# A hand-written instruction order re-planned from its last third on, with the last row tile stored in halves

## The chip, the cores and the metric

The kernel runs on one core of a Trainium2 chip. A core has five engines with an instruction stream each: TensorE (PE in the rows, its weight loads PEld), VectorE (DVE), ScalarE (ACT), GpSimd (POOL) and SyncE (SP), which here only issues DMAs. Each stream runs in order; between streams there are semaphores. The metric is device time in microseconds (us), from the first to the last instruction of the core and what lies around it. Three runs of the kernel before took 441.34, 442.01 and 442.62 us; the median, 442.01 us, is the time before.

## The reference

A linear attention and a feed-forward layer. What is computed, cut to its core:

```python
q_s = exp(q - max(q, -1));  q_s /= sum(q_s, -1) + 1e-9        # 8 x 8 x 576 x 64
k_s = exp(k - max(k, 2));   k_s /= sum(k_s, 2) + 1e-9
kv = einsum('bhsd,bhse->bhde', k_s, v)
x = einsum('bhsd,bhde->bhse', q_s, kv)                        # -> 4608 x 512
h = x @ w_in                                                  # 512 -> 1024
sm = exp(h - max(h, -1));   sm /= sum(sm, -1) + 1e-9
solu = h * sm
ln = (solu - mean) / sqrt(var + 1e-6) * g_ln
out = ln @ w_out                                              # 1024 -> 512
```

## The kernel before

The 4608 rows are 36 row tiles of 128 rows (`tiles`): four main tiles for each of the 8 batches, and one tile for each pair of batches that holds 64 remaining rows of both ("rests"). A tile's name is its batch and its place in it: `6_0` is tile 27, `7_2` is tile 33, `5_4` is tile 26 (a rest). float32 operands of the matmuls are split into a high and a low float16 part, and a product is three matmuls.

From tile 13 on, two tiles are one work (twins, `late_rests` too): `hidden_twin` computes the hidden layer of both with seven block products in place of eight (lines 726 to 784). A block product is 6 matmuls of 128x512 (L734). Of a twin, `t2` is the hidden tile of the second row tile and `t1` that of the first. The order is: product 11 onto `t2`, product 12 onto `t1`; a copy of `t2` (`vw`, L172 on ScalarE or L174 on VectorE); products s2 and s1; copies; s3 and s4; reduces on VectorE (L770, L772); the last product, 22 with t4, onto `t2`; its reduce (L777). There are two hidden tiles in PSUM at a time (`h`, two slots), so a twin's first product waits for the last read of the hidden tiles of the twin before: `L842` (in `hidden`, one tile) or `L939` (in `hidden_pair`, both tiles, one instruction each). Before `L842` stand, for its tile, the maximum (L772 or L777 and L779), its absolute value `am` (L829), `pi` (L832), its power `p` (L835, always POOL) and `ph` (L838); before `L939` the same for two tiles in 128x2 instructions (L919, L927, L929, L890, L935).

Five pairs (tiles 27, 29, 31, 33 and 26; `SPLIT_OUT`) are also projected by seven block products (`pair_products`, L1049, 12 matmuls of 128x256 each, three accumulators x, y, z) and scaled and stored by `pair_rows`. Other tiles are projected by `project` (L1113, 6 matmuls of 128x512 a step, 24 a tile). Between u and uT lies a DMA transpose on SP (L859, L898).

Nothing is scheduled by a tool: the table `ORDER` is a list of steps and `in_turns` runs one generator step for each, so the order in that list is the order in every engine's stream. `K6` is the next step of the keys of batch 6, `Q7a` of queries, `x27` of the attention of tile 27, `h22` of a tile's hidden layer after the products, `H27` of a twin's products, `U27` of `hidden_pair`, `O27` of its products, `E27` of its rows, `o20` of a tile's projection, `TO` of the blocks of the output weights (L1009 to L1021); `.v` puts the step's movable instruction on VectorE in place of its default, ScalarE or GpSimd, and `*3` repeats it. `SLOTS` says which buffer each tile takes.

`pair_rows` has 11 steps: rr; a copy of x; y plus that; four scalings; `scaled_onto` twice; `stored(1)` and, last, `stored(0)`, each one or two DMAs (two for a rest, of 64 rows).

Of the kernel before, what the change touches and what calls it, by code (L numbers as in the profile page):

```python
# [17 lines left out]
P = 128  # L18
# [5 lines left out]
REST_TWINS = 5, 7  # L24
SPLIT_OUT = (27, 29, 31, 33, 26)
# [78 lines left out]
def linear_attention_solu_ffn(ctx: ExitStack, tc: tile.TileContext, q, k, v, w_in, w_out, g_ln, out):  # L104
# [7 lines left out]
    nc = tc.nc  # L112
# [942 lines left out]
    def pair_rows(row_tiles):  # L1055
# [20 lines left out]
        def stored(i):  # L1076
            for rows, dst in destinations(row_tiles[i]):
                nc.sync.dma_start(out=dst, in_=out_rows[rows, i])
# [5 lines left out]
        scaled(0, right, "y")  # L1084
        yield
        scaled(0, left, "x")
        yield
        scaled(1, right, "y")
        yield
        scaled_onto(1)  # L1090
# [160 lines left out]
```

## Time and profile before

| | |
|---|---|
| median of three runs | 442.01 us (441.34 to 442.62) |
| the profiled execution | 440.85 us, of it the span 439.1 us, granted TensorE clock 0.997 |
| busy in the span | PE 417.4 us (95%), DVE 385.5 us (88%), ACT 323.4 us (74%), POOL 316.1 us (72%) |
| chain that ended last | PE 73%, POOL 8%, ACT 8%, DVE 6% |
| DMA | 77.93 MB; HBM read 36.70 MB, written 9.44 MB |

PE's busy share is read together with the views by stage: the first 66 us hold most of its idle time, and the end of the span, after the last matmul, the rest. A row of a timeline gives the start, the length, the engine and line, and, in brackets, how long the engine was idle just before and what ended that.

### The profile page before, as it was taken

What the parts mean: (1) busy time and instruction counts of PE and PEld (TensorE: products, weight loads), DVE (VectorE), ACT (ScalarE), POOL (GpSimd) and SP (SyncE); (2) the same over time, 40 slices, a digit from 0 to 9 for tenths busy, and PEclk for the clock granted to TensorE, in tenths of its full rate; (3) what the DMA queues carried; (4) which work ended last, traced back from release to release, by engine and by line L of the source; (5) the groups of instructions that cost most, each with busy time, mean ns of one, the idle gap of its engine ahead of it and who ended that gap; (6) DMA issues with size and microseconds to landing.
All of it is one profiled execution on the core that took longest, in us unless ns stands there. A gap on an engine that the chain in (4) does not pass through costs nothing.

```text
span 439.1 us, 9202 instructions
## 1 busy us (share of the span) xinstructions
PE 417.4 (95%) x3441; PEld 218.1 (50%) x3441; DVE 385.5 (88%) x765; ACT 323.4 (74%) x555; POOL 316.1 (72%) x336
## 2 busy tenths in 40 slices
PE   2798899999999999999999999999999999999995
PEld 1444344454454444544544445445444445666885
DVE  5999999999898998889988869999999998988952
ACT  3799998696796689878875677768685686785920
POOL 4206983889998879859966888886939897778340
PEclk9999999999999999999999999999999999999998
DMA  8989788489799696499996568994533665379982
GB/s 277 409 306 315 154 152 233 91 206 245 173 223 184 150 192 135 90 224 217 186 251 146 126 147 188 247 215 95 78 72 82 111 144 104 63 172 188 231 204 73
DMA packets 182620, 77.93 MB, mean 177 GB/s; under 512 B 162088, under 2 KB 171312, under 8 KB 182576
## 3 DMA queue, kind: packets, MB, share of 16 engines
q1 hardware_dynamic: 182576, 77.35, 77.0%
q8 instruction: 27, 0.44, 0.4%
q14 instruction: 17, 0.14, 0.1%
HBM read 36.70 MB, written 9.44 MB: 105 GB/s over the span
## 4 chain that ended last, share of the span: by engine, by line
PE 73%; POOL 8%; ACT 8%; DVE 6%; issue 3%; DMA 1%; ACTq 0%; POOLq 0%; DVEq 0%
PE o L1113 24%; PE h L734 18%; PE h L811 12%; PE kv L471 3%; PE x L666 3%; PE o_2y L1049 2%; PE o_0y L1049 2%; PE o_0x L1049 1%; PE o_2z L1049 1%; PE o_0z L1049 1%; PE o_2x L1049 1%; POOL qm L523 1%; POOL r L882 1%; POOL qhl L548 1%; POOL am L829 1%
## 5 line engine op out<-in xcount | busy, mean ns | idle before, releaser
L1113 PE MATMUL o<-wo,uT 128*128 128x512 f16 x624 | 141.4, 379 | 0.0
L1113 PEld LDWEIGHTS <-uT 128*128 128x128 f16 x624 | 60.3, 98 | 72.7 <-issue 1.6
L811 PE MATMUL h<-wi,xT 128*128 128x512 f16 x240 | 54.4, 379 | 0.0
L734 PE MATMUL h<-wt,split 128*128 128x512 f16 x198 | 46.2, 379 | 0.9 <-ACT vw L172 0.9
L734 PEld LDWEIGHTS <-split 128*128 128x128 f16 x264 | 25.5, 98 | 31.7 <-issue 2.5
L457 POOL TENSOR_TENSOR km<-km,kb 128x1152 f32<-128x1152 f32 x12 | 33.6, 2808 | 4.9 <-ACT kb L435 3.2
L811 PEld LDWEIGHTS <-xT 128*128 128x128 f16 x240 | 23.1, 98 | 27.5 <-issue 0.6
L548 POOL TENSOR_TENSOR qhl<-qm,qhl 128x512 f16<-128x512 f32 x24 | 28.8, 1220 | 3.0 <-ACT qhl L172 2.9
L734 PE MATMUL h<-wi,xT 128*128 128x512 f16 x132 | 30.8, 379 | 0.1
L734 PEld LDWEIGHTS <-xT 128*128 128x128 f16 x198 | 19.1, 98 | 23.6 <-issue 1.8
L803 PE MATMUL h<-iw,xT 128*128 128x512 f32 x64 | 29.5, 602 | 1.2 <-ACT e L866 1.2
L541 POOL TENSOR_TENSOR qm<-qm,qrec 128x1024 f32<-128x1024 f32 x13 | 25.6, 1966 | 6.3 <-DVE qrec L532 6.0
L523 POOL TENSOR_TENSOR qm<-qm,qnmx 128x1024 f32<-128x1024 f32 (+1 forms) x14 | 25.3, 1810 | 5.7 <-DVE qnmx L521 5.5
L825 ACT ACTIVATE e<-h,nm,hs 128x1024 f32<-128x1024 f32 x20 | 24.0, 1202 | 0.5
L852 POOL TENSOR_TENSOR u<-e,u 128x1024 f16<-128x1024 f32 x8 | 17.6, 2200 | 9.0 <-ACT u L172 4.6
L1126 ACT ACTIVATE os<-o,rr 128x512 f32<-128x512 f32 x23 | 15.7, 684 | 11.0 <-PE o L1113 7.9
L521 DVE TENSOR_REDUCE qnmx<-qm 128x16 f32<-128x1024 f32 (+1 forms) x17 | 19.2, 1147 | 4.3 <-DMA qm<-in_q_dram 4.3
L829 POOL TENSOR_SCALAR am<-top 128x1 f32<-128x1 f32 x21 | 10.9, 518 | 15.2 <-DVE top L819 14.2
L525 ACT ACTIVATE qm<-qm 128x1024 f32<-128x1024 f32 (+1 forms) x17 | 17.1, 1003 | 5.9 <-POOL qm L523 5.9
L471 PE MATMUL kv<-vm,km 64*64 64x65 f32 x1152 | 19.3, 219 | 2.0 <-ACT km L459 0.9
L459 ACT ACTIVATE km<-km 128x1152 f32<-128x1152 f32 x16 | 18.5, 1163 | 3.4 <-POOL km L457 3.2
L471 PEld LDWEIGHTS kv<-vm,km 64*64 64x64 f32 x1152 | 18.0, 134 | 5.8 <-issue 3.3
(330 smaller groups left out, 1057.6 us busy)
## 6 DMA issues: line engine op xcount, KB each, us to landing
out_dram<-os SPq DMA_DIRECT2D x32, 256.0 KB, 3.0
km<-in_k_dram SPq DMA_DIRECT2D x7, 1152.0 KB, 7.3
vm<-in_v_dram SPq DMA_DIRECT2D x28, 288.0 KB, 4.3
qm<-in_q_dram SPq DMA_DIRECT2D x7, 1024.0 KB, 6.7
wo<-in_moe_w_in_dram SPq DMA_DIRECT2D x4, 512.0 KB, 8.8
w_in<-in_moe_w_in_dram SPq DMA_DIRECT2D x4, 512.0 KB, 9.2
wo<-in_moe_w_out_dram SPq DMA_DIRECT2D x4, 512.0 KB, 4.4
w_out<-in_moe_w_out_dram SPq DMA_DIRECT2D x4, 512.0 KB, 6.8
```

Of the source, the lines that this page charges most:

```text
L457: on(nc.gpsimd).tensor_tensor(km[:, ns], km[:, ns], wide, op=ALU.subtract)
L471: nc.tensor.matmul(o, km[half, n, c], vm[half, n, c], start=(m == 0 and c == 0), stop=(m == 1 and c == KC - 1))
L521: nc.vector.tensor_reduce(shaped(nmx), x, axis=AX.X, op=ALU.max, negate=True)
L523: on(nc.gpsimd).tensor_tensor(x, x, wide(nmx), op=ALU.add)
L541: on(nc.gpsimd).tensor_tensor(x, x, wide(rec), op=ALU.mult)
L548: on(nc.gpsimd).tensor_tensor(lo, y, hi, op=ALU.subtract)
L734: nc.tensor.matmul(out, lefts[left](s, i), right_block(right, r, i), start=(n == 0 and not onto), stop=(n + 1 == len(terms)), skip_group_c ...
L803: nc.tensor.matmul(h[:, ns], xT[:, kc], iw[kc][:, ns], start=(i == 0), stop=(i == NP - 1))
L811: nc.tensor.matmul(h[:, ns], xT[:, t, kc], wi[:, s, kc, ns], start=(i == 0), stop=(i == len(terms) - 1))
L825: nc.scalar.activation(e, h, AF.Exp, bias=nm, scale=hs, accum_out=z)
L1049: nc.tensor.matmul(accs[acc], t[:, j, first + f], out_block(right, s, f), start=(f == n == 0 and not onto), stop=(f + 1 == NF // 2 and n = ...
L1113: nc.tensor.matmul(o, uT[:, j, f], wo[:, s, f, cols], start=(f == 0 and j == 0 and s == 0), stop=(f == NF - 1 and j == 1))
```

## The change

It is a change to the tables, and one of a few lines to `pair_rows`.

- `ORDER` is the same list of steps for the first 1168 of its 1819 entries; in them 24 steps have another engine (19 gain `.v`, 5 lose it), most of them small steps of one tile's hidden layer, three of them in the first 170 steps: the copy of the first turned queries goes from ScalarE to VectorE, the cast of the last quarter of the first values (`V03`) the other way, and one step of `h1`.
- From entry 1169 on the steps stand in another order with other engines. Of the new order the last pair is tile 33 with 34's place taken by the rests (26) before it: `E33` ends the list where `E26` ended it. `SLOTS` follows.
- `LAST = 33`: in `pair_rows` of that pair the left half of the first tile's rows is stored as soon as it is scaled, and the last step stores the right half alone. That is one step and one DMA more for pair 33.

```diff
+LAST = 33
@@ ORDER, an early line @@
-    "K0*3 w2 K0 P Q0b V03.v Q0a Q0c.v Q0c Q0a K0.v K0 K0.v K0*2 Q0c Q0c.v w3 w2 K0*2 w3*2 Q0a x0 K0 w0*2 x0 w1*2 "
+    "K0*3 w2 K0 P Q0b.v V03 Q0a Q0c.v Q0c Q0a K0.v K0 K0.v K0*2 Q0c Q0c.v w3 w2 K0*2 w3*2 Q0a x0 K0 w0*2 x0 w1*2 "
@@ ORDER, its end @@
-    "E26 E33*2 O26*2 E26.v E26*3 "
+    "U33.v U33 U33.v E31.v O26*2 U33*2 U33.v U33*3 E26*2 E31*2 E26 O26 E26.v E26 O33 E31 O26 U33*2 U33.v U33 E26*2 "
+    "O33 E33.v*2 O33*2 E33 E33.v*2 O33 E33 E33.v E33 O26 O33*2 E26*2 E33.v E33*3 "
@@ pair_rows @@
-        def stored(i):
+        ending = tiles.index(row_tiles[0]) == LAST
+
+        def stored(i, cols=slice(0, DM)):
             for rows, dst in destinations(row_tiles[i]):
-                nc.sync.dma_start(out=dst, in_=out_rows[rows, i])
+                nc.sync.dma_start(out=dst[:, cols], in_=out_rows[rows, i, cols])
...
         scaled(0, left, "x")
         yield
+        if ending:
+            stored(0, left)
+            yield
         scaled(1, right, "y")
...
-        stored(0)
+        stored(0, right if ending else slice(0, DM))
         yield
```

TensorE's stream has the same 4897 entries in both, in another order; VectorE's has 730 in place of 716. Lines of the changed kernel are 2 higher than before up to `pair_rows` and 4 to 7 higher behind it.

Place A is the start of twin 27 (`h6_1` is its `t2`, `h6_0` its `t1`). ScalarE's stream before, up to the copy `vw6_0` that the s2 product waits for (`e5_3` is the exponential of tile `5_3`, the second of the twin before it; `nmu5_3` comes from that tile's last read of its hidden tile):

```order
L844 ACTIVATE nmu5_3_4314<-s15_3_4312 128x1
L172 CAST u5_2_4310<-e5_2_4200 128x1024
L525 ACTIVATE qr6_3813<-qr6_3813 128x512
L502 COPY bd3_83<-bd3_83 64x256
L172 COPY vw6_0_4335<-h6_1_4336 128x512
```

There the exponential pass L848 over `e5_3` comes only after the copy. ScalarE's stream of the change, over the same stretch:

```order
L174 CAST u5_2_4258<-e5_2_4207 128x1024
L504 COPY bd3_83<-bd3_83 64x256
L502 ACTIVATE bd3_83<-kvn7_4172,s_kv7_4230 64x256
L846 ACTIVATE nmu5_3_4291<-s15_3_4289 128x1
L174 CAST qhl7_0_4310<-qm7_3848 128x4x2x64 x2
L850 ACTIVATE e5_3_4250<-e5_3_4250,nmu5_3_4291 128x1024
L174 COPY vw6_0_4293<-h6_1_4294 128x512
```

The copy now stands behind the pass over `e5_3` (L850, before L848), which needs `nmu5_3`. In TensorE's stream the whole projection `o5_00` (24 matmuls) now stands between the products of `h6_1` and of `h6_0`, where they were neighbours; ahead of the product of `h6_1` there now stand, behind the last product of twin 24, 18 matmuls of `o4_30` alone, where 36 matmuls of projections stood (and ahead of that last product 6 of `o4_30`, where the 16 small ones of `x6_2` stood); and the attention `x7_0` (16 matmuls) stands ahead of the last product of twin 27.

At the same place, POOL's stream before, up to the power and `ph` of tile `5_2`, which its last read (L842) needs, and that read frees the hidden tile that `h6_1` takes:

```order
L181 TENSOR_TENSOR rr4_3_4216<-r4_3_4155,osc_70 128x1
L523 TENSOR_TENSOR qm7_3811<-qm7_3811,qnmx7_0_3891 128x8x128
L1013 TENSOR_TENSOR ob00_3694<-ob01_3823,ob00_3694 128x1024
L835 TENSOR_TENSOR p5_2_4242<-pi5_2_4225,mone_73 128x1
L838 TENSOR_SCALAR ph5_2_4244<-p5_2_4242,hs5_3654 128x1
```

The block `ob00` stands just ahead of the power `p5_2`. POOL's stream of the change, from that block on:

```order
L1015 TENSOR_TENSOR ob00_3728<-ob01_3897,ob00_3728 128x1024
L884 TENSOR_TENSOR r4_3_4086<-var4_3_3866,mhalf_71 128x1
L183 TENSOR_TENSOR rr4_3_4090<-r4_3_4086,osc_70 128x1
L854 TENSOR_TENSOR u5_1_3987<-e5_1_3899,u5_1_3987 128x1024
L837 TENSOR_TENSOR p5_2_4241<-pi5_2_4239,mone_73 128x1
L840 TENSOR_SCALAR ph5_2_4243<-p5_2_4241,hs5_3654 128x1
```

The subtraction `u5_1` now stands just ahead of the power, and the block three further up.

Place B is the end of twin 27, where pair 27's last reads (L939) free the hidden tiles for twin 29. VectorE's stream before, from the reduces of twin 27 to the first of these reads:

```order
L772 ISA h6_0_4343,tops6_0_4371<-h6_0_4343,vw6_0_4335,top6_0_0_4367 128x512
L772 ISA tops6_0_4371 128x1
L777 TENSOR_REDUCE top6_0_3_4370<-h6_1_4336 128x1
L179 TENSOR_SCALAR rr5_2_4439<-r5_2_4406,osc_70 128x1
L1013 TENSOR_TENSOR ob11_3883<-ob11_3883,ob00_3694 128x1024
L779 TENSOR_SCALAR tops6_0_4371<-top6_0_3_4370,top6_0_1_4368 128x1
L919 TENSOR_TENSOR nm26_0_4471<-tops6_0_4371,hs6_3854 128x2
L927 SCALAR_TENSOR_TENSOR pi26_0_4478<-nm26_0_4471 128x2
L890 RECIPROCAL p2s6_0_4481<-pi26_0_4478 128x2
L935 TENSOR_TENSOR ph26_0_4483<-p2s6_0_4481,hs6_3854 128x2
L939 SCALAR_TENSOR_TENSOR e6_0_0_4474,nmu26_0_4492<-h6_0_4343,ph26_0_4483,e6_0_0_4474 128x1024
```

Behind the last reduce (L777) two instructions of other work stand ahead of the read. VectorE's stream of the change, from just behind the last reduce:

```order
L781 TENSOR_SCALAR tops6_0_4399<-top6_0_3_4398,top6_0_1_4396 128x1
L921 TENSOR_TENSOR nm26_0_4489<-tops6_0_4399,hs6_3846 128x2
L929 SCALAR_TENSOR_TENSOR pi26_0_4511<-nm26_0_4489 128x2
L931 TENSOR_SCALAR pi26_0_4511<-pi26_0_4511 128x2
L892 RECIPROCAL p2s6_0_4514<-pi26_0_4511 128x2
L1021 TENSOR_TENSOR ott3_4469<-ob01_3897,ott3_4469 128x1024
L872 TENSOR_SCALAR z15_3_4520<-z5_3_4251,p5_3_4282 128x1
L937 TENSOR_TENSOR ph26_0_4523<-p2s6_0_4514,hs6_3846 128x2
L550 TENSOR_TENSOR qhlr6_4476<-qr6_3850,qhlr6_4476 128x4x64 x2
L709 SCALAR_TENSOR_TENSOR sums7_0_4505<-x7_0_0_4446,xT7_0_4504 128x256
L711 SCALAR_TENSOR_TENSOR xT7_0_4504<-x7_0_0_4446,xT7_0_4504 128x256
L941 SCALAR_TENSOR_TENSOR e6_0_0_4492,nmu26_0_4549<-h6_0_4346,ph26_0_4523,e6_0_0_4492 128x1024
```

Between the reciprocal and the read there now stand six instructions more (`ott3`, `z15_3`, two of `qhlr6`, `sums7_0`, `xT7_0`), and `pi26_0` has its second instruction on VectorE. Ahead of the last reduce the cast `split6_2` is gone and a product of the queries, `qm7` (L543), has come; the block that stood behind it (L1013) stands ahead of it. In TensorE's stream 36 matmuls of projections stand between twin 27's last product and twin 29's first, where 30 stood.

Place C is the end of SP's stream. Before, the last stores (`os` are the rows to be stored; 5_4 is the rest, 7_2 is tile 33):

```order
L898 DMA_TRANSPOSE uT5_4a_5453<-u5_4a_5450 128x16x128
L898 DMA_TRANSPOSE uT5_4b_5485<-u5_4b_5482 128x16x128
L898 DMA_TRANSPOSE uT5_4c_5543<-u5_4c_5502 128x16x128
L898 DMA_TRANSPOSE uT5_4d_5548<-u5_4d_5545 128x8x128
L1078 DMA out_0_dram<-os7_0_5406 128x512 x2
L1078 DMA out_0_dram<-os7_2_5500 128x512 x2
L1078 DMA out_0_dram<-os5_4_5617 64x512 x4
```

The last four entries are the two tiles of the rests, two DMAs each. SP's stream of the change, its end:

```order
L900 DMA_TRANSPOSE uT7_2c_5568<-u7_2c_5565 128x16x128
L1082 DMA out_0_dram<-os7_0_5356 128x512 x2
L900 DMA_TRANSPOSE uT7_2d_5618<-u7_2d_5570 128x8x128
L1082 DMA out_0_dram<-os5_4_5519 64x512 x2
L1082 DMA out_0_dram<-os7_2_5645 128x256
L1082 DMA out_0_dram<-os5_4_5519 64x512 x2
L1082 DMA out_0_dram<-os7_2_5645 128x512
L1082 DMA out_0_dram<-os7_2_5645 128x256
```

Pair 33 now comes last in three DMAs, and the last entry is one DMA of 128x256 in place of the two of 64x512 that stored a rest tile.

## Rows read from the trace of the kernel before

**Rows 1.** Windows: stretch, length, busy us (instructions) by engine, clock, DMA share, GB/s.
```profile
core 0: us, PE busy (x) PEld busy (x) DVE busy (x) ACT busy (x) POOL busy (x), PEclk, DMA share, GB/s
...
320.00:330.00 10.00, 9.09 (x43) 4.09 (x42) 9.75 (x20) 8.36 (x14) 2.39 (x5) 1.00 0.35 79
330.00:340.00 10.00, 9.48 (x45) 4.18 (x44) 9.42 (x19) 5.36 (x8) 9.43 (x7) 1.00 0.37 84
```
**Rows 2.** Timeline of PE, 305 to 345 us: start, us, what [idle before].
```profile
309.04 0.97 PE L666 MATMUL x<-qT,bd 128*64 128x256 f16 x16
...
319.13 2.75 PE L734 MATMUL h<-wi,xT 128*128 128x512 f16 x12
322.79 2.75 PE L734 MATMUL h<-wt,split 128*128 128x512 f16 x12 [0.91 <-ACT vw L172]
...
327.97 1.46 PE L734 MATMUL h<-wt,split 128*128 128x512 f16 x6
...
331.24 1.46 PE L734 MATMUL h<-wt,xT 128*128 128x512 f16 x6 [0.52 <-DVE top L770]
332.53 6.64 PE L1113 MATMUL o<-wo,uT 128*128 128x512 f16 x30
339.01 2.75 PE L734 MATMUL h<-wi,xT 128*128 128x512 f16 x12
```
**Rows 3.** Timeline of all engines at place A, 310 to 318 us.
```profile
310.62 0.21 DVE L832 TENSOR_SCALAR pi<-am,hs 128x1 f32<-128x1 f32 x1
...
311.72 3.33 POOL L1013 TENSOR_TENSOR ob<-ob,ob 128x1024 f32<-128x1024 f32 x1
...
315.02 0.80 POOL L835 TENSOR_TENSOR p<-pi,mone 128x1 f32<-128x1 f32 x1
...
316.03 0.42 DVE L709 SCALAR_TENSOR_TENSOR xT<-x,xT 128x256 f16<-128x256 f32 x1
...
316.36 1.28 DVE L842 SCALAR_TENSOR_TENSOR e<-h,ph,e 128x1024 f32<-128x1024 f32 x1
```
**Rows 4.** Timeline of DVE at place B, 329 to 341 us.
```profile
330.44 0.69 DVE L770 CUSTOM_DVE_ANT_0 h<-h,vw 128x512 f32<-128x512 f32 x1
...
331.05 1.30 DVE L174 CAST split<-sums 128x1024 f16<-128x1024 f32 x1
...
333.67 1.76 DVE L1013 TENSOR_TENSOR ob<-ob,ob 128x1024 f32<-128x1024 f32 x1
...
336.50 0.90 DVE L935 TENSOR_TENSOR ph<-p2s,hs 128x2 f32<-128x2 f32 x1
337.52 1.28 DVE L939 SCALAR_TENSOR_TENSOR e<-h,ph,e 128x1024 f32<-128x1024 f32 x1
```
**Rows 5.** Groups by form: out<-in, count, busy us, mean ns, idle before.
```profile
L852 DVE TENSOR_TENSOR u<-e,u 128x1024 f16<-128x1024 f32 x4 | 4.9, 1233 | 0.0
L548 DVE TENSOR_TENSOR qhl<-qm,qhl 128x512 f16<-128x512 f32 x4 | 2.6, 687 | 0.0
L174 DVE COPY vm<-wi 128x576 f32<-128x576 f32 x1 | 0.7, 744 | 0.0
...
L852 POOL TENSOR_TENSOR u<-e,u 128x1024 f16<-128x1024 f32 x8 | 17.6, 2200 | 9.0 <-ACT u L172 4.6 <-DVE u L174 4.4
```
**Rows 6.** Timeline of the end of the span, 434.5 us on.
```profile
434.64 0.48 DVE L1074 SCALAR_TENSOR_TENSOR os<-o_4z,rr,os 128x256 f32<-128x256 f32 x1 [0.90 <-PE o_4z L1049]
```
**Rows 7.** Timeline of SP's queue, 435.6 us on, and the store's line from 434.
```profile
435.15 1.11 SPq L1078 DMA_DIRECT2D out_dram<-os  x2
...
L1078 SPq DMA_DIRECT2D out_dram<-os x4: 467/543/587, 433.8 to 435.7; - x4
...
DMA to landing us min/median/max: 2.2/2.3/2.4
```
**Rows 8.** Timeline of all engines, 417 to 418 us.
```profile
417.41 2.46 POOL L972 TENSOR_TENSOR u_4c<-su,u_4c 128x1024 f16<-128x1024 f32 x1 [4.99 <-ACT u_4c L172]
...
417.81 2.08 DVE L949 SCALAR_TENSOR_TENSOR z<-zz,p2s 128x2 f32<-128x2 f32 x1
```

108 rows, old and new, of tables (ORDER, SLOTS) are left out of this document.

## The prediction

> **What bounds the kernel now.** I read the busy table first, then the windows, PE's timeline in the stretch that the change touches, the streams of VectorE, POOL and ScalarE behind each wait found there, and the end of the span. The busy table gives PE 417.4 of 439.1 us. In the windows PE is busy 10.00 of 10.00 us in nearly all stretches from 70 to 430 us; the two with most idle time in the last third are 320 to 330 with 9.09 and 330 to 340 with 9.48 [rows 1]. [...] So the reader is to see one engine that is nearly always at work, and a table of steps can win only what PE still waits. In that stretch PE's timeline has two waits: 0.91 us for a copy of a hidden tile by ScalarE, and 0.52 us for a maximum by VectorE [rows 2], together 1.43 us. VectorE is almost as full beside it, 9.75 and 9.42 of 10 us [rows 1], so an instruction more ahead of something PE needs is paid for as soon as PE's cover is used up. After the last matmul there is a tail: VectorE's last scaling starts at 434.64 [rows 6] and the span ends at 439.1, about 4.5 us later.
>
> **The sum.** It starts from the profiled execution, 440.85 us, of which 1.75 us lie outside the span. The median of three runs is 1.16 us longer, 442.01; I carry the difference over to the median.
>
> *Steps that keep their place.* 24 of them change engine. From 70 us on PE's own work covers them, and PE's total is the same 4897 entries. In the first 70 us, where PE does wait, two of the three are a swap between ScalarE and VectorE: the cast of values leaves VectorE (0.74 us [rows 5]) and a copy of about the same size comes. I take 0; without cover it would be at most that 0.7 us either way.
>
> *The wait of 0.91 us.* It ended with the copy `vw6_0`, which had only one product of 6 matmuls (12 of them start at 319.13, and the next row follows at 322.79 [rows 2]) to hide behind. A matmul of 128x512 costs 0.216 us: 30 of them from 332.53 to 339.01 [rows 2]. The change puts the 24 matmuls of `o5_00` between the two products, 5.2 us of cover. But ScalarE's stream now has the copy behind the pass over `e5_3`, which needs a last read of VectorE. That read must be over before `h6_0` may start as well, so about one pass and one copy are left exposed against one product of 1.3 us. Bounds: 0 and the old 0.91. I take 0.4 us, about the middle: 0.5 us gained.
>
> *The wait of 0.52 us.* It was for the reduce ahead of the last product. The attention `x7_0` now stands between, 16 small matmuls; their like takes 0.97 us [rows 2]. That is more than the wait, so it goes: 0.5 us gained, 0 if the copy before it is late by that much.
>
> *A new wait ahead of twin 27.* `h6_1` needs the last read of `h5_2`. Before, from the end of product s4 (309.04 at the latest) to the first product at 319.13 PE had 10.1 us of other work [rows 2]; the read, L842, ended at 316.36 + 1.28 = 317.64 [rows 3], so 1.5 us were spare. Now that cover is 30 matmuls, 6.5 us. The chain took 8.6 us before, but in it the power on POOL stood from 310.83, where `pi` ended, to 315.02 behind one block of 3.33 us [rows 3]: without that, 4.4 us. Now `pi` comes some 0.9 us later, behind four small instructions on the keys (so 5.3), and POOL has the subtraction `u5_1`, 2.2 us [rows 5], just ahead. Free POOL: 5.3 against 6.5, no wait. `u5_1` wholly in the way: 7.5, a wait of 1.0. The block as well: up to 10.8, a wait of 4.3. I take 0.3, nearest the first two; both ends stay in the range.
>
> *A new wait ahead of twin 29 (place B).* Before, from the end of product s3 (327.97 + 1.29 = 329.26) to the first product at 339.01 PE had 9.75 us [rows 2]. VectorE began its reduce 1.2 us late, at 330.44, and was done with the first last read at 337.52 + 1.28 = 338.80 [rows 4]: 0.2 us spare. Now PE's cover is: product s4 and the last product 2.6, the attention 0.97, 36 matmuls 7.8, in all 11.4 us, 1.6 more. VectorE loses the cast of 1.30 [rows 4], a small one of 0.2 and two short idle times of some 0.3; it gains a product `qm7` and the block `ott3` at 1.23 each (the nearest row of that size on VectorE [rows 5]), two halves `qhlr6` at between half of 0.687 and all of it [rows 5], two pieces at 0.42 [rows 3], and three small ones of 0.2. That is 4.6 to 5.3 less 1.8, less some 0.3 by which neighbours overlap: 2.5 to 3.2. Against 1.6 + 0.2 a wait of 0.7 to 1.4 is left. If `ph` falls from its 0.90 us [rows 4] to a small instruction's 0.2 it is 0 to 0.7. If the two large ones are stretched as the block was (1.76 in place of 1.23 [rows 4, 5]), another 1.1: 2.5 at most. I take 0.8.
>
> *The other four pairs* stand in a new order too. PE's timeline has no bracket at any of them now. I take 0; the bounds of B hold for each.
>
> *The tail.* The last store was two DMAs, 1.11 us from the first's start to the second's end [rows 7], and each lands 2.2 to 2.4 us after its start [rows 7]. It becomes one of 128 rows of half length. One issue of 0.5 us goes; the landing stays, since it hardly varies in these rows, and the smaller DMA has as many bytes as each of the two. So 0.5 us gained; 0.1 if pieces of 1 KB land slower than those of 2 KB by the spread that the rows show. The extra store of the left half is issued before that, in SP's idle time; behind it in the queue stand only stores. Of the last pair's transposes the last one, `uT7_2d`, now waits behind two stores, 1.1 us by the same row; only the very last block product needs it, with the other products of that pair and of the rests in between, so it costs nothing, and 1.1 us if they do not cover it.
>
> Sum: -0.5 - 0.5 + 0.3 + 0.8 - 0.5 = -0.4 us. 440.85 - 0.4 = 440.45, and on the median 442.01 - 0.4 = 441.6 us. About 0.3%, 1.3 us, is what a measurement of this kernel can tell from no change, so this is none.
>
> [...] At 417.81 an instruction of VectorE on two numbers a partition took 2.08 us; it ended at 419.89, and POOL's subtraction, begun at 417.41, at 419.87 [rows 8]. [...]
>
> **Rivals.**
>
> 1. *All of PE's waits in the stretch go* (chance 0.33). For it: each of the two has more cover now, and the new waits at A and B are differences of sums with an error as large as they are. Against it: VectorE is over 94% busy there. Then -1.43 - 0.5 = -1.9: 440.1 us.
>
> 2. *VectorE becomes the bound at the ends of the pairs* (chance 0.25). The place is the last read L939 of each pair, which frees the hidden tiles for the next twin. At place B two large instructions are now queued ahead of it; each that starts beside a POOL instruction is stretched, as `ph` and the 128x2 product were [rows 4, 8]. Price: 2.5 us at B in place of my 0.8, and half of that, some 1.1 us, at two of the other four pairs, +3.9 in all: 445.5 us. With half of the stretching it is +1.9, 443.5, which I take. It decides from 1.7 us of waits over those in my sum. For it: 0.2 us spare at B before. Against it: at the other ends of pairs nothing in the trace waits.
>
> **How the numbers follow.** The forecast, waits that change place and a tail shorter by one DMA, has 0.42: 441.6, by its own bounds 440.7 to 443.2. Rival 1 has 0.33 at 440.1, rival 2 has 0.25 at 443.5 and beyond. A tenth is left out on either side: 439.7 to 444.4. Faster by over 0.3%, below 440.7: rival 1 and a little of the forecast, 0.36. Slower by over 0.3%, above 443.3: most of rival 2, 0.23. Within: 0.41.
>
> **What would show it.** In the profile of the changed kernel: PE's count and busy time as before; a wait of under 0.9 us for the copy `vw6_0`; no wait for the maximum ahead of its last product; a wait ahead of twin 27's first product with L842 as its releaser, and one ahead of twin 29's with L939; one DMA last in SP's queue, and a span that ends some 4 us after the last matmul in place of 4.6. The prediction is wrong if PE's waits behind 262 us add up to under 0.5 us or over 3 us, or if the first 260 us differ by more than 0.7 us.

## The result, and the profile after

| | before | changed |
|---|---|---|
| median us (lowest to highest) | 442.01 (441.34 to 442.62), 5 runs | 437.82 (437.55 to 438.30), 5 runs |
| profiled execution, span | 440.85, 439.1 | 437.55, 435.7 |
| PE, VectorE, ScalarE, POOL busy | 417.4, 385.5, 323.4, 316.1 | 416.9, 380.8, 326.9, 311.0 |

The ratio is 0.9905, with a 95% interval of 0.9890 to 0.9919: 4.2 us faster. The forecast was 441.6 within 439.7 to 444.4. The prediction was wrong, in size and in what it called likeliest.

The windows of the changed kernel that answer to [rows 1]:

```profile
core 0: us, PE busy (x) PEld busy (x) DVE busy (x) ACT busy (x) POOL busy (x), PEclk, DMA share, GB/s
320.00:330.00 10.00, 9.85 (x47) 4.40 (x45) 9.76 (x17) 9.30 (x16) 7.66 (x9) 1.00 0.62 127
330.00:340.00 10.00, 10.00 (x60) 4.49 (x58) 9.83 (x23) 7.71 (x15) 4.86 (x4) 1.00 0.36 83
```

VectorE is as full as it was; PE no longer waits for it in this stretch. ScalarE has 17.0 us of work in these 20, where it had 13.7. PE's timeline in the same stretch (start, us, what [idle before]), against [rows 2]:

```profile
310.79 1.46 PE L736 MATMUL h<-wt,xT 128*128 128x512 f16 x6
312.08 4.05 PE L1120 MATMUL o<-wo,uT 128*128 128x512 f16 x18
315.96 1.46 PE L736 MATMUL h<-wi,xT 128*128 128x512 f16 x6
317.26 5.34 PE L1120 MATMUL o<-wo,uT 128*128 128x512 f16 x24
322.44 1.46 PE L736 MATMUL h<-wi,xT 128*128 128x512 f16 x6
324.05 2.75 PE L736 MATMUL h<-wt,split 128*128 128x512 f16 x12 [0.15 <-ACT vw L174]
...
332.81 1.47 PE L736 MATMUL h<-wt,xT 128*128 128x512 f16 x6
334.12 7.93 PE L1120 MATMUL o<-wo,uT 128*128 128x512 f16 x36
341.89 2.75 PE L736 MATMUL h<-wi,xT 128*128 128x512 f16 x12
```

Of the 0.91 us for the copy 0.15 are left, the 0.52 us for the maximum are gone, and neither new wait that I had forecast is there: no bracket at 315.96 (place A) nor at 341.89 (place B). Place A from all engines (against [rows 3]):

```profile
311.45 2.13 POOL L854 TENSOR_TENSOR u<-e,u 128x1024 f16<-128x1024 f32 x1
...
313.53 0.56 POOL L837 TENSOR_TENSOR p<-pi,mone 128x1 f32<-128x1 f32 x1
...
314.48 1.28 DVE L844 SCALAR_TENSOR_TENSOR e<-h,ph,e 128x1024 f32<-128x1024 f32 x1 [1.26 <-POOL ph L840]
```

The subtraction `u5_1` holds the power back from 312.07, where `pi` was done, to 313.53; the read still ends at 315.76, 0.2 us ahead of the product. Place B on VectorE, with POOL's block beside it (against [rows 4]):

```profile
331.86 1.22 DVE L1015 TENSOR_TENSOR ob<-ob,ob 128x1024 f32<-128x1024 f32 x1
...
333.16 3.28 POOL L1015 TENSOR_TENSOR ob<-ob,ob 128x1024 f32<-128x1024 f32 x1 [3.10 <-DVE ob L1015]
...
335.77 0.68 DVE L921 TENSOR_TENSOR nm<-tops,hs 128x2 f32<-128x2 f32 x1
...
336.97 1.21 DVE L1021 TENSOR_TENSOR ott<-ob,ott 128x1024 f16<-128x1024 f32 x1
...
338.22 0.15 DVE L937 TENSOR_TENSOR ph<-p2s,hs 128x2 f32<-128x2 f32 x1
...
339.62 1.28 DVE L941 SCALAR_TENSOR_TENSOR e<-h,ph,e 128x1024 f32<-128x1024 f32 x1
```

Before, POOL's large instructions stood beside the block (333.67) and beside `ph` (336.50), and not beside `nm`:

```profile
331.76 2.58 POOL L1019 TENSOR_TENSOR ott<-ob,ott 128x1024 f16<-128x1024 f32 x1
...
335.58 0.16 DVE L919 TENSOR_TENSOR nm<-tops,hs 128x2 f32<-128x2 f32 x1
...
336.24 2.27 POOL L548 TENSOR_TENSOR qhl<-qm,qhl 128x512 f16<-128x512 f32 x2
```

The block takes 1.22 us in place of 1.76 and `ph` 0.15 in place of 0.90, and POOL's large instructions no longer stand beside them. `nm` takes 0.68 in place of 0.16: it now stands beside POOL's block, and ends with it, at 336.45. The first read ends at 340.90, 1.0 us ahead of PE. The end of the span, against [rows 6, 7]:

```profile
432.25 0.48 DVE L1076 SCALAR_TENSOR_TENSOR os<-o_2z,rr,os 128x256 f32<-128x256 f32 x1 [0.83 <-PE o_2z L1051]
432.76 0.34 SPq L1082 DMA_DIRECT2D out_dram<-os  x1
```

From this last scaling to the span's end it is 3.45 us, against 4.46. The last DMA lands 1.9 us after its start, against 2.2 and 2.4.

At 133 us PE was 0.76 us ahead of the kernel before, and from 184 to 262 us it was still 0.55 to 0.6 ahead. There was one stall in the middle of these products of keys and values before, and none there in the changed kernel:

```profile
133.09 0.45 PE L471 MATMUL kv<-vm,km 64*64 64x65 f32 x13 [0.58 <-issue]
```

```profile
130.30 2.48 PE L473 MATMUL kv<-vm,km 64*64 64x65 f32 x144
```

### The profile page after: what moved, and what is told of

It reads as the page before. It is cut to its first block, busy times and chain, and to the rows that moved or that the text cites. A ratio compares the mean times of both kernels' runs of the same rounds, so it can differ in the third digit from the quotient of the medians.

```text
span 435.7 us, 9209 instructions
## 1 busy us (share of the span) xinstructions
PE 416.9 (96%) x3441; PEld 218.8 (50%) x3441; DVE 380.8 (87%) x784; ACT 326.9 (75%) x549; POOL 311.0 (71%) x323
## 4 chain that ended last, share of the span: by engine, by line
PE 80%; DVE 6%; POOL 4%; issue 3%; ACT 3%; DMA 2%; SPq 1%; POOLq 0%; DVEq 0%; ACTq 0%
PE o L1120 26%; PE h L736 20%; PE h L813 12%; PE kv L473 4%; PE x L668 3%; PE h L805 2%; PE o_0y L1051 2%; PE o_2y L1051 2%; POOL ob L1011 1%; PE o_2z L1051 1%; PE o_0x L1051 1%; PE o_2x L1051 1%; PE o_0z L1051 1%; DMA qm<-in_q_dram 1%; DMA vm<-in_v_dram 1%
## 5 line engine op out<-in xcount | busy, mean ns | idle before, releaser
L459 POOL TENSOR_TENSOR km<-km,kb 128x1152 f32<-128x1152 f32 x12 | 34.9, 2916 | 10.4 <-issue 5.8
L550 POOL TENSOR_TENSOR qhl<-qm,qhl 128x512 f16<-128x512 f32 x26 | 31.4, 1228 | 5.9 <-ACT qhl L174 5.8
L525 POOL TENSOR_TENSOR qm<-qm,qnmx 128x1024 f32<-128x1024 f32 (+1 forms) x13 | 23.8, 1833 | 5.9 <-DVE qnmx L523 5.9
L543 POOL TENSOR_TENSOR qm<-qm,qrec 128x1024 f32<-128x1024 f32 x11 | 22.4, 2038 | 5.8 <-DVE qrec L534 5.7
L837 POOL TENSOR_TENSOR p<-pi,mone 128x1 f32<-128x1 f32 x26 | 16.3, 627 | 5.5 <-DVE pi L834 4.2
L530 DVE TENSOR_REDUCE qsum<-qm 128x16 f32<-128x1024 f32 (+1 forms) x17 | 19.5, 1146 | 0.3 <-ACT qm L527 0.2
```

Of the source, the lines that this page charges most:

```text
L459: on(nc.gpsimd).tensor_tensor(km[:, ns], km[:, ns], wide, op=ALU.subtract)
L525: on(nc.gpsimd).tensor_tensor(x, x, wide(nmx), op=ALU.add)
L530: nc.vector.tensor_reduce(shaped(sums), x, axis=AX.X, op=ALU.add)
L543: on(nc.gpsimd).tensor_tensor(x, x, wide(rec), op=ALU.mult)
L550: on(nc.gpsimd).tensor_tensor(lo, y, hi, op=ALU.subtract)
```

## The experiments

The profile left three questions: what the early engines are worth, what the waits at A and B hang on, and what the tail is made of. Medians of one session share its runs of the kernel before; those were 441.76 (first four), 442.22 (next four), 442.23 (next four) and 442.58 (last two).

**1. The kernel before again.** No edit.

> The kernel before, unchanged. Its one profiled execution (440.85 us) lies below all five timed ones (441.34 to 442.62, median 442.01), while the changed kernel's profiled one (437.55) is its fastest of five. That is 0.9 us of the 4.2 us between the medians which no row of the two profiles shows. Theory V (stalls of the old order vary from execution to execution, and the profiled one was a lucky one): the times again 441.3 to 442.6; this profile differs from the first in PE's waits behind 70 us, which added up to 2.2 us there (0.58 at 132.5, 0.23 at 178.7, 0.91 at 321.9, 0.52 at 330.7); some of them another size or another place by over 0.3 us, and the span by as much. Rival F (everything is fixed; a timed run is just longer by a constant): the same four waits to within 0.1 us and the same span of 439.1.

Measured: 442.19 (440.96 to 442.65), span of the profile 440.5. The two large waits are back at 0.92 and 0.52, the stall at 132.6 is 0.71. Two waits are new:

```profile
155.93 5.34 PE L811 MATMUL h<-wi,xT 128*128 128x512 f16 x24 [0.33 <-ACT e L866]
...
184.92 0.50 PE L471 MATMUL kv<-vm,km 64*64 64x65 f32 x17 [0.36 <-issue]
```

So theory V holds: the order's own waits are fixed, and what varies lies ahead of 190 us. The execution that I had started from was a lucky one, with little of it; the profile of 12, of the same order up to the end, has the same three waits ahead of 190 us as this one (0.72, 0.34 and 0.39).

**2 and 3. The early engines alone, and the rest alone.**

```diff
@@ 2: the kernel before; 24 steps like these @@
-Q0b V03.v
+Q0b.v V03
@@ 3: the changed kernel, the same 24 steps @@
-Q0b.v V03
+Q0b V03.v
```

> The kernel before with the engines of the changed one in the first 1168 steps (24 steps), and nothing else. Theory E (the early engines are worth what the first 270 us gained): 0.6 to 0.7 us less, 441.3 to 441.4, PE's stall of 0.58 us at 132.5 gone, the waits of 0.91 and 0.52 behind 320 us and the tail of 4.5 us as they were. Rival (that stall is not tied to the engines; it comes and goes): same time within 0.3 us, 442.0, with a stall of such a kind somewhere in 70 to 270 us or without.

> The changed kernel with the old engines in the first 1168 steps; the later order, the last pair and the store in halves are the new ones. Theory L (later order and tail make all of it, the early engines nothing): 437.8, ratio to before 0.990 to 0.991. Rival E (early engines worth 0.6 to 0.7): 438.4 to 438.5, with the stall of 0.58 us near 132.5 back. Whatever comes, early part and late part should add up: this run's gain and that of the kernel with the early engines alone together 4.2 us.

Measured: 444.27 (443.72 to 445.18) for the early engines alone, ratio 1.0051 (1.0037 to 1.0064), and 439.55 (438.83 to 441.11) for the rest, ratio 0.9945 (0.9926 to 0.9964). They don't add up: +2.5 and -2.2 against -4.2 for both. In 2 the stall at 132.5 is gone, as theory E has it, but VectorE is late for the old order's later steps:

```profile
281.87 1.46 PE L734 MATMUL h<-wi,split 128*128 128x512 f16 x6 [1.63 <-DVE vw L174]
283.99 1.46 PE L734 MATMUL h<-wt,xT 128*128 128x512 f16 x6 [0.67 <-DVE top L770]
```

In 3 the stall is back, 0.82 us at 132.6, and no such waits come.

**4. The last tile stored whole.**

```diff
-LAST = 33
+LAST = 99
-E33.v E33.v O33 O33 E33 E33.v E33.v O33 E33 E33.v E33
+E33.v E33.v O33 O33 E33 E33.v O33 E33 E33.v E33
```

> The changed kernel without the halves: the last row tile, 33's first, is stored whole by one DMA of 128x512 behind the last scaling, one step fewer. Theory H (the halves carry the shorter landing: 1.9 us in the changed kernel for the last DMA of 128x256, 2.2 and 2.4 us for the two of 64x512 before): landing 2.3 us or more, the time 0.3 to 0.6 us longer, 438.1 to 438.4. Rival O (it is the one DMA in place of two alone, with nothing else in the queue): landing 1.9, the time within 0.1 us of the changed kernel, 437.8 to 437.9.

Measured: 437.97 (437.62 to 438.36). In its profile the last DMA lands 2.4 us after its start, and the tail is 436.4 - 432.44 = 3.96 us. Theory H holds for the rows, 0.5 us; the medians show 0.15 of it, which is within their spread. The edit does one thing more: with a step fewer, one scaling of the left half (`os7_2`) goes from VectorE to ScalarE. It is over before the last scaling, from which the tail is counted.

**5. One load earlier in the old order.**

```diff
-V31 Q2c Q2c ... x8 V30 S1
+V31 V30 Q2c Q2c ... x8 S1
```

> The kernel before with one load moved: the last quarter of batch 3's values (V30, 288 KB) is issued right behind V31 at about 111 us, where SP idles until 115, in place of at 124.5 between the transposes. Engines and the order of all other steps stay. PE's stall of 0.58, 0.71 and 0.82 us near 132.5 in the three profiles with the old early engines lies in the middle of the products of keys and values; in each, PE goes on 1.4 us behind the end of a packet of 16 KB of the instruction queue q8 (ends 131.64, 131.91, 132.03, PE goes on at 133.09, 133.31, 133.41), and that packet starts as the transposes' packets run out. Theory F (PE waits for its own instructions, whose fetch comes late behind a full DMA stretch): with 288 KB less ahead of it the packet starts 0.7 us or more earlier, the stall is gone with the old engines, and the time falls by 0.5 to 0.7 us, to about 441.2. Rival (the stall belongs to ScalarE's and VectorE's streams, as the new early engines removed it): the stall stays, 441.8 as before.

Measured: 441.25 (440.59 to 441.88), ratio 0.9978 (0.9965 to 0.9990). The packet starts at 128.75, and the stall is gone with the old engines:

```profile
130.39 2.33 PE L470 MATMUL kv<-vm,km 64*64 64x65 f32 x144
```

Theory F's outcome came, with the packet 1.93 us earlier than in the kernel before (130.68). In the four profiles with the stall this packet starts at 130.68 to 131.03, in the other twelve at 130.0 or earlier. Queue q8, of the kind `instruction` in the profile, brings 27 packets of 16 KB in a run. That they are PE's is my estimate: its 3441 matmuls and 3441 weight loads are some 255 to each packet, and the 144 small matmuls of this stretch with their 144 weight loads, 288 instructions, are over in 2.33 us. That PE stood still for want of a packet is inferred from these times; no row shows it. From 120 to 130 us, ahead of the packet, the DMA share of the kernel before was 1.10. For the load itself PE does not wait: V30, issued at 124.52 in the kernel before, landed 3.9 us later, ahead of these products, and the row of the matmul behind the stall has no releaser (`issue`).

**6 and 7. The 24 early changes cut at step 1000.**

```diff
@@ 6: the kernel before with the first 19; not with these five @@
 o15.v ... h19 ... h19 ... h20.v ... h20.v
@@ 7: the changed kernel, the last five set back @@
-o15 ... h19.v ... h19.v ... h20 ... h20
+o15.v ... h19 ... h19 ... h20.v ... h20.v
```

> The kernel before with the first 19 of the 24 early engine changes (up to step 897), without the last five (steps 1050 to 1143, tile layers 19, 20 and projection 15). With all 24 it was 2.5 us slower, with new PE waits of 1.63 and 0.67 at 280 to 283 us and 0.81 at 404. Theory N (the last five belong to the later order and hurt the old one; the 19 remove the stall at 132.5): 441.0 to 441.3, no such waits, the old ones of 0.91 and 0.52 as before. Rival (the waits at 280 come from the 19, through a shift that lasts): 443.5 or more, with waits at 280.

> The changed kernel with the last five of its early engine changes (steps 1050 to 1143) set back. Theory N (these five belong to the new later order): a new wait of PE behind 262 us and 438.5 or more. Rival (the new order stands with either): 437.8 within 0.2. With all 24 set back it was 439.55, of which the stall at 132.5 was 0.8.

Measured: 441.84 (440.86 to 442.46), ratio 0.9997 (0.9983 to 1.0011), and 437.75 (437.33 to 438.36). In 6 the stall is gone and the waits at 280 us with it; but one of 0.81 us at 403 is there, as in 2, so that nothing is gained. The five make the waits at 280 in the old order; the 19 make the one at 403 (one profile each), and theory N's 441.0 to 441.3 is missed. In 7 nothing changes: theory N is wrong there. The new order takes either; the old one gains from neither.

**8. At place B, one block back to POOL.**

```diff
-U27 U27.v U27.v TO.v TO TO
+U27 U27.v U27.v TO TO TO
```

> The changed kernel with one block at place B given back to POOL: the low half of ott3 (128x1024, 1.21 us on VectorE at 336.97, the largest of the six instructions put ahead of the last reads L941). In the changed kernel the first of these reads ended 1.0 us before PE's next product, so that nothing waited. Theory by count (the prediction's: what is queued on VectorE adds up): VectorE reaches the read 1.2 us earlier, at about 338.4, and the time stays at 437.8. Theory by what runs beside it (an instruction of VectorE on two numbers a partition took 0.68 and 0.90 us, over with POOL's block, in place of 0.15 to 0.2): the block goes to POOL, POOL's next block runs beside ph, ph takes 1 us or more, the read is late, and PE waits 0.5 to 1.5 us ahead of the product of twin 29: 438.3 to 439.3.

Measured: 438.34 (437.72 to 439.65). VectorE and POOL there:

```profile
336.38 2.35 POOL L1015 TENSOR_TENSOR ob<-ob,ob 128x1024 f32<-128x1024 f32 x1
336.47 2.27 DVE L929 SCALAR_TENSOR_TENSOR pi<-nm 128x2 f32<-128x2 f32 x1
...
340.60 1.28 DVE L941 SCALAR_TENSOR_TENSOR e<-h,ph,e 128x1024 f32<-128x1024 f32 x1
```

VectorE has 1.21 us less to do and comes to the read 0.98 us later. An instruction on two numbers a partition (`pi`, not the `ph` that the theory named) took 2.27 us and ended with POOL's block, at 338.74. PE does not wait at this read yet (the spare 1.0 us is used up), but 0.37 and 0.29 us later on. The count is wrong here: what went with the longer time is what ran beside it. That is shown by the rows; the medians, 438.34 of four runs and 437.82, do not tell the two kernels apart.

**9. More cover for the copy in the old order** (with 5's load).

```diff
-TO.v TO.v H27 H27 H27 H27 ... x29 o21 o21 h24.v
+TO.v TO.v H27 H27 H27 o21 H27 ... x29 o21 h24.v
```

> The kernel before with V30's load earlier (441.25 by itself) and one more move at place A: one step of the projection of tile 5_0's row before (6 matmuls, 1.3 us), which stood behind twin 27's product s1, now stands between its first two products and s2, where PE waited 0.92 us for the copy. Theory W (PE's waits are a bill of single items, as the prediction's sum has them): the 0.92 us go, the 0.51 us for the maximum at 331 stay, 440.3. Theory D (behind the copy VectorE is the bound: it began the reduce L770 1.2 us after PE's product was done): what PE gains at the copy it waits more for the maximum, 0.51 becomes 1.0 to 1.4, and the time stays at 441.0 to 441.3.

Measured: 441.21 (440.69 to 442.14), as 5 alone. The wait at the copy is gone, and the next one has it all:

```profile
323.52 2.75 PE L733 MATMUL h<-wt,split 128*128 128x512 f16 x12
...
331.63 1.46 PE L733 MATMUL h<-wt,xT 128*128 128x512 f16 x6 [1.47 <-DVE top L769]
```

Theory D: 0.51 + 0.92 = 1.43, measured 1.47. In the old order VectorE was the bound here, and PE's two waits were one.

**10. Three loads earlier in the changed kernel** (V30 as in 5, and V43 and V41).

```diff
-h9 h12 h12 ... x15 V43 h10 V41 h12.v
+h9 h12 V43 V41 h12 ... x15 h10 h12.v
```

> The changed kernel with three loads of values issued where SP idles: V30 behind V31 (111 us), V43 and V41 behind the transposes at 157 to 160 us in place of 173 and 174. In all profiles a stall without a releaser in the products of keys and values at 182 to 185 us (0.10 to 0.56 us, but for the first one of the kernel before) ends 1.4 us behind the end of a packet of q8. Theory F (instruction fetch behind a full DMA stretch): that packet starts at 179.7 or earlier in place of 180.7, the stall goes, and the time is 437.4 to 437.7. Rival (that packet's time is set by PE's place in its program, not by the DMA load): packet and stall as before, 437.8.

Measured: 437.39 (437.05 to 437.55), ratio 0.9892 (0.9876 to 0.9908). The stall at 182.6 stays, 0.40 us, and its packet starts at 180.38: the rival's outcome, at this place. Stall and packet go together here too: in the three of the sixteen profiles in which it starts at 180.20 or earlier (the first of the kernel before, 3 and 13) there is no stall, and in the others, from 180.38 on, one of 0.10 to 0.67 us. The time is 0.4 us below the changed kernel's, which is not enough to tell them apart over two sessions.

**11. The later part alone, with the load earlier.** Edit 3 and edit 5.

> The kernel with the new later order and the old early engines (439.55; 438.83 to 441.11), and V30's load earlier. Theory F (what the 24 early engine changes are worth under the new order is the fetch that comes in time): no stall at 132.6, 437.9 to 438.4, and no run at 440 or above. Rival (they are worth something by themselves behind 133 us too): 438.6 to 439.0.

Measured: 438.50 (438.16 to 439.46), ratio 0.9925 (0.9912 to 0.9939); no stall at 132.6. The load gives 1.05 us of the 1.73 between 439.55 and 437.82 (three sessions). Between the two theories: a wait of 0.33 us at 154.5, which the old early engines have in other runs too, and a stall of 0.67 at 183.5 remain.

**12. Halves at the old end.** The three edits of `pair_rows` with `LAST = 26`, and one `E26` more.

> The kernel before with the store in halves for its own last pair, the two rest tiles: the left halves of the last one are stored as soon as they are scaled (two DMAs of 64x256), the last step stores two DMAs of 64x256 in place of two of 64x512. The tail from the last scaling's start to the span's end was 4.4 to 4.5 us in four profiles of this ending, 3.45 in the changed kernel, 3.96 there without halves. Theory S (half comes from the smaller last DMA, half from there being one): 3.9 to 4.0, the last landing at 1.9 to 2.0 us, the time 0.4 to 0.5 us less than before, which the spread of the times hardly shows. Rival (landing does not go by size): 4.4 to 4.5.

Measured: 441.83 (440.85 to 443.13), ratio 0.9994 (0.9984 to 1.0004). The last two DMAs land 1.9 and 2.0 us after their starts, and the tail is 440.2 - 436.10 = 4.1 us: 0.35 of the 1.0. Theory S holds roughly: with half the bytes the last step lands some 0.4 us sooner, and one issue in place of two is the rest. The rows of these DMAs were also halved, from 2 KB to 1 KB, so that bytes and length of a row are not told apart.

**13 and 14. Copies between VectorE and ScalarE at place B.** TensorE's order is untouched in both.

```diff
@@ 13: edit 9, and two copies to ScalarE @@
-H27.v H27 H27 h24 h24 x29 x29 h25 h25.v
+h24 h24 x29 x29 h25 H27 H27 H27 h25
@@ 14: the changed kernel, three copies to VectorE @@
-Q7c.v h25 R7 ... h25.v H27 H27 H27 H27 x29
+Q7c.v h25.v R7 ... h25.v H27.v H27 H27 H27 x29.v
```

> The kernel before with V30's load earlier and the projection step as cover (441.21; PE's wait at the copy gone, the one for the maximum L770 grown from 0.51 to 1.47 us), and now two copies of VectorE ahead of that maximum on ScalarE, as the new order has them: vw6_0 from the second hidden tile and the cast of u5_3, 0.68 us each. TensorE's stream is untouched. Theory D (VectorE is the bound at this place): the maximum starts 1.2 to 1.4 us earlier, PE's wait falls from 1.47 to 0.1 to 0.3, and the time to 440.0. Rival (ScalarE is as full and takes its place, or the next wait does, at the last reads L939 that end 0.2 us ahead of PE): the time stays within 0.3 of 441.2.

> The changed kernel with three copies at the same place put back on VectorE, where the old order had them: the cast of u5_3, the copy vw6_0 from the second hidden tile (0.68 us each) and the cast of split6_2 (1.30). Nothing else moves; TensorE's stream is untouched. VectorE's maximum L772 ended 0.9 us ahead of PE's last product of twin 27, the first last read L941 1.0 us ahead of the next twin. Theory D: the maximum is 1.3 us later, the read 2.6, so that PE waits 0.4 us at the one and 1.2 more at the other, 1.6 in all: 439.4. Rival (where these copies run does not matter; the new order gains by PE's cover alone): 437.8 within 0.3.

Measured for 13: 440.32 (439.63 to 440.97), ratio 0.9943 (0.9927 to 0.9959), where 9 had 0.9983 (0.9974 to 0.9992).

```profile
329.50 1.46 PE L733 MATMUL h<-wt,xT 128*128 128x512 f16 x6 [0.50 <-DVE top L769]
...
337.64 2.75 PE L733 MATMUL h<-wi,xT 128*128 128x512 f16 x12 [0.21 <-DVE e L938]
```

PE's wait falls from 1.47 to 0.71 (0.50 and 0.21), and the median by 0.9 us (by the ratios to the kernel before 1.8). Measured for 14: 443.34 (441.64 to 444.11), 5.5 us more than the changed kernel (by the ratios 4.6), where theory D had 1.6:

```profile
326.80 2.66 POOL L1021 TENSOR_TENSOR ott<-ob,ott 128x1024 f16<-128x1024 f32 x1 [0.40 <-ACT ott L174]
...
327.39 2.62 DVE L176 CAST u<-e 128x1024 f16<-128x1024 f32 x1
...
333.90 0.68 DVE L176 COPY vw<-h 128x512 f32<-128x512 f32 x1
...
334.63 2.72 PE L736 MATMUL h<-wi,split 128*128 128x512 f16 x6 [3.76 <-DVE vw L176]
```

The cast of 0.68 us begins beside POOL's instruction and takes 2.62: it ends at 330.01, 0.55 after POOL. PE then waits for the copy `vw6_0`, which stands on VectorE behind that cast and other work, and not, as theory D had it, for the maximum and the last read. The wait of 3.76 us costs more than itself. By windows (the eighth column is the granted clock):

```profile
326.00:330.00 4.00, 4.00 (x20) 1.82 (x19) 3.97 (x4) 2.84 (x4) 3.60 (x3) 1.00 0.80 150
330.00:334.00 4.00, 0.86 (x5) 0.29 (x3) 3.93 (x9) 0.00 (x0) 0.61 (x2) 0.87 0.35 131
334.00:338.00 4.00, 3.37 (x14) 1.24 (x13) 3.86 (x7) 0.74 (x1) 0.70 (x1) 0.50 0.69 131
338.00:342.00 4.00, 4.00 (x25) 1.60 (x22) 2.19 (x7) 3.14 (x8) 2.58 (x1) 0.78 0.00 0
```

While PE idled the granted clock fell: it was 1.00 up to 330, 0.87 on the mean of the window with the wait, 0.50 from 334 to 338, 0.55 from 338 to 340, and 1.00 from 340 to 342. From this product to the projections it is 340.59 - 334.63 = 5.96 us, in the changed kernel 334.12 - 330.52 = 3.60. So theory D is right in kind, wrong in the place of the wait, and mis-sized by the 1.9 us that the cast beside POOL's instruction took longer and by the 2.4 us more from this product to the projections, at the lower granted clock.

## Why the prediction was wrong

The sum ran from 440.85 to 440.45, the profile gave 437.55, and the medians differ by 0.9 us more. By its terms:

| step | forecast us | measured us |
|---|---|---|
| wait for the copy `vw6_0` | -0.5 | -0.76 |
| wait for the maximum | -0.5 | -0.52 |
| new wait, place A | +0.3 | 0 |
| new wait, place B | +0.8 | 0 |
| tail | -0.5 | -1.0 |
| other waits behind 262 us | 0 | +0.17 (at 305) |
| PE's waits in the first 260 us | 0 (at most 0.7) | -0.6 |
| PE's own busy time | 0 | -0.56 |
| profiled execution to median | carried, 1.16 | 1.16 before, 0.27 after: -0.9 |

The terms miss by 3.8 us together, and none alone is most of it: the waits at B and A are 1.1 of it, the carry 0.9, the first 260 us 0.6, PE's busy time 0.56, the tail 0.5, the copy 0.26, and the wait at 305 takes 0.17 back. PE's busy time is left open: it lay between 416.75 and 417.90 us in the eight profiles of the old order and between 416.05 and 416.86 in the seven others without 14.

**The step that failed is the new wait at place B, with the one at A.** It came out of "That is 4.6 to 5.3 less 1.8", a count of what is queued on VectorE with each instruction at its own time. At B a wait of 0.8 us was forecast, and the read was done 1.0 us ahead of PE. From its reduce (330.44 before, 331.19 after) to the end of the first read VectorE took 8.36 us before and 9.71 after: 1.35 more, not 2.5 to 3.2. Its instructions' own times grew by 2.37 us, where the count has 3.1 to 3.8; that they overlap, or idle less, gave 1.03, where I took 0.6. The block and `ph` lost 0.54 and 0.75 us [rows 4] and `nm` gained 0.52, together 0.77 less, about what 2.37 lies under the low end of the count. The first two are shorter, and `ott3` (2.58 us from 331.76 before) and the product `qhl` (from 336.24) no longer run on POOL beside them: what I counted as a load on VectorE had stood beside its longer instructions on POOL. I had named the case, "If `ph` falls from its 0.90 us [rows 4] to a small instruction's 0.2 it is 0 to 0.7", and not taken it. Experiment 8 puts that work back: VectorE has less to do and is later.

The 2.08 us of an instruction on two numbers a partition, over with POOL's subtraction [rows 8], I had counted against the change (rival 2). Experiment 8 has its like, 2.27 us, over with POOL's block; at the block and `ph`, which lost 0.54 and 0.75 us with no such instruction of POOL beside them, the same spoke for the change. VectorE also came to its reduce earlier against PE, 0.67 us behind the start of product s4 (330.52) and not 1.18, which is 0.5 of the 1.8 us between the wait forecast and the time to spare. ScalarE has copies that were VectorE's, and 13 and 14 show that this is worth PE time there. At A, `u5_1` held the power up by 1.46 us, between the two cases that I had, and the read was in time by 0.2; no run was made on A alone.

**A second error lay under it.** I took PE's waits as a bill of single items. In 9 one was paid and the next took all of it. The result, that both went, is rival 1's (chance 0.33, 440.1); its reason, more cover on PE, is not enough: in the old order cover for the copy alone gains nothing (9), and in the new one, with all its cover, three copies back on VectorE cost more than the gain (14). How much of the gain is cover's and how much the copies' was not separated.

**The tail** was mis-sized by its landing, "the landing stays, since it hardly varies in these rows". It goes with what is under way at the end, or with the length of its rows, which these runs do not tell apart: 2.4 us for one DMA of 256 KB (4), 2.2 and 2.4 for two of 128 KB [rows 7], 1.9 for one of 128 KB, 1.9 and 2.0 for two of 64 KB (12). Rows are of 2 KB in the first two and of 1 KB in the last two.

**The early steps** were costed at nothing with PE's work as cover. The cover held; what went with them was an earlier start of a packet of queue q8, 129.99 in place of 130.68, and the end of PE's stall of 0.58 us. In 5 an earlier packet (128.75) and no stall came together as well; in 10 the packet at 180.38 and the stall of 0.40 us both stayed. That PE waits for the packet is inferred from these times. Which of the 19 changes brings it forward was not tried.

**The carry to the median** assumed that what varies does so alike in both. The profile before was a lucky execution (1), so that 1.16 us was luck and no property of the kernel. Five runs each spread over 1.28 us before and 0.75 changed; in the larger sets of later sessions the kernel before spread over 1.5 to 3.3. To one change the old order is the more sensitive, by 2, 6 and 7: the last five of the early changes cost it 2.4 us (444.27 and 441.84) and the new order nothing (437.82 and 437.75). What made three of the six runs of 3 longer than the others by 1.4 to 2.3 us is open.

**What held:** PE's order as the same entries, VectorE's chain at A (6.4 us against a cover of 6.6, forecast 5.3 to 7.5), the wait for the maximum, and the sign that I had set for being wrong, "The prediction is wrong if PE's waits behind 262 us add up to under 0.5 us": they add up to 0.32.

## What to carry to other kernels

Ask of each wait of the bounding engine who else is late behind it: giving it cover pays only if the stream that it waits for is not itself the bound. When work moves between VectorE and POOL, count what it stood beside, not only its own time; a small instruction in the chain is worth moving away from a large one on POOL (`nm`, `ph` and `pi` took 0.15 to 0.16 us by themselves and 0.68, 0.90 and 2.27 beside one). An order that waits little in one execution may be at the edge of several waits, so profile it more than once before a sum starts from it.

## What the hardware showed that I had not expected

- TensorE stood still in a run of small matmuls, for 0.58 to 0.82 us near 132.5, in all four profiles that have the old early engines and the load V30 at its old place, and in none of the twelve others. A packet of queue q8 started at 130.68 to 131.03 in the four and at 130.0 or earlier in the twelve (5); that it is what TensorE waited for is inferred from these times.
- A cast of 128x1024 from float32 to float16 on VectorE took 0.64 to 0.70 us 102 times, but each of the 33 in the sixteen profiles that began while a TENSOR_TENSOR of 512 or 1024 numbers a partition was running on POOL ended 0.55 us after that one, whenever it began, and so took 0.70 to 2.62. The cast of 1.30 us that the sum takes away at place B is one of them (POOL's instruction ended at 331.80, the cast at 332.35). The reduces of 128x512 over a hidden tile, 176 in these profiles, took 0.68 to 0.69 us, and 127 of them began beside a POOL instruction of over 1 us.
- In 14 TensorE waited 3.76 us in a stretch that it had filled. The granted clock was 1.00 from 326 to 330 us, 0.50 from 334 to 338 and 1.00 again from 340 to 342.
